# A new order for the attention loop of an attention, mixture-of-experts and SwiGLU kernel

## Chip, cores and metric

The kernel runs on one core of a Trainium2 chip. The metric is the device time of one execution in microseconds. All three stages run in one launch, and the input layouts are prepared before it. Engines are written PE (TensorE, its weight loads apart as PEld), DVE (VectorE), ACT (ScalarE), POOL (GpSimd) and SP (SyncE, which here only issues DMAs).

## Reference

```python
# attention, B=4 H=8 S=576 D=64
scores = (1/sqrt(D)) * q @ k.T
rel = pos[:, None] - pos[None, :]
scores = where((rel >= 0) & (rel < 64), scores, -1e9)
attn = softmax(scores)
x = (attn @ v) -> [2304, 512]
# mixture of experts, N=2304 D=512 E=8 F=1024, top 2
noisy = x @ w_gate + log1p(exp(x @ w_noise)) * noise
top2, weights = softmax over the two largest
y = sum over the token's two experts of weight * (relu(x @ w1[e]) @ w2[e])
# SwiGLU, d_ff=1536
out = (silu(y @ w_gate2) * (y @ w_val2)) @ w_out2
```

## The kernel before

The 2304 tokens are 18 tiles (`NT`) of 128. Three stages follow each other: the attention loop with the gate logits and the routing, the eight experts in order of their token counts, and SwiGLU in six blocks of 384 tokens. Each engine runs its instructions in the order in which the code emits them, so the order of calls in the loop over `T` is the order on each engine. Tiles named with a tag have a fixed number of buffers (`bufs`); a buffer is written again only when all readers of its last content are done.

The attention loop, on which the change bears, works on several tiles at once. In iteration `T`:

- `trans_p(T)` transposes the softmax numerators of tile T on PE (8 matmuls into `ptp`, PSUM banks 4 and 5); ACT copies them to `pt`; DVE forms the reciprocal row sums `rr`.
- `qk(T+2, ...)` adds the mask (2 matmuls with `identb`) and the scores (32 matmuls of 64 rows, `sc`) of tile T+2, in three parts: head pairs 0 and 1, then 2, then 3. The scores of two tiles in work lie in four banks, 0 to 3.
- `softmax(T+2)`: DVE takes row maxima `nm` and scales them to `nms`; ACT makes 8 exponentials.
- `pv(T)`: 32 matmuls into `xp` (bank 6), DVE scales them to `xs`, and a DMA stores `xs` to `x_d` in DRAM, from which tokens are gathered for the experts later.
- `win_v(T+2)`: POOL builds the shifted V block `vw` (2 buffers).
- `trans_x(T-1)` transposes `xs` into `xtp` (also bank 6), ACT copies it to `xt`; `logits(T-2)` multiplies by the gate weights into `misc` (bank 7) and DVE copies to `lts`; `gates(T-2)` holds `trans_l`, which turns `lts` on PE, and a DVE copy to `lg`.
- `route_some(ns)` emits some DVE steps of the routing of a group of five tiles (softplus, top 2, positions in the experts, index lists); a group is opened when `gates` has done its last tile, which is in iterations 6, 11 and 16.
- `split_pair` (iterations 3 to 10): POOL splits one raw weight pair of the first expert into a high part (L114) and the rest (L117), 1024 columns each; SP loads the next raw pair (3 buffers).
- `load_super` loads q, k and v for two tiles (SP); `link_k` is a DVE copy of the last K block of the former pair of tiles into the middle place of the new K tile.

After the loop, a list `TAIL` orders the rest of the attention with the first matmuls of the first expert between it.

Of the kernel before, what the change touches and what calls it, by code (L numbers as in the profile page):

```python
# [7 lines left out]
F32 = mybir.dt.float32  # L8
# [6 lines left out]
ALU = mybir.AluOpType  # L15
# [24 lines left out]

TAIL = ("P16", "L14", "Q14", "R302", "X15", "R1500", "G0", "P17", "V16", "L15", "G1", "W", "V17", "Q15", "R9000", "X16",
        "M0", "L16", "X17", "R9000", "R500", "Q16", "R1", "R2500", "L17", "M2", "W", "R500", "M1", "Q17", "W", "M3",
        "R1500", "E", "R700", "M5", "M6", "M4", "R9000", "E", "W", "R9000", "Y0", "Y1", "M7")
TAIL2 = ("Y2", "Y3")
# [7 lines left out]
def tile_attention_moe_swiglu(ctx: ExitStack, tc: tile.TileContext, qh, kh, vh, wgn, noise, w1h, w2h,  # L54
# [14 lines left out]
    def bank(i, name, shape=None):  # L69
        return ps.tile(shape or [128, 512], F32, name=name, tag=f"b{i}")  # L70
# [32 lines left out]
    def split_pair(pool):  # L103
        j = st["split"]
        if j >= NPAIR:
            return
        while st["load"] < min(j + 3, st["lim"]):
            load_pair()
        st["split"] += 1
        w = pool.tile([128, 2, 1024], F32R, name=f"wp{j}", tag="w")  # L110
        pairs[j] = w
        r = raws.pop(j)
        if st["split"] <= PSPL:
            nc.gpsimd.tensor_scalar(w[:, 0, :], r, 1.0, 0.0, op0=ALU.mult, op1=ALU.add)  # L114
# [166 lines left out]
    with ExitStack() as ac:  # L281
        ap = ac.enter_context(tc.tile_pool(name="ap", bufs=1))

        def load_super(s):
            qt = ap.tile([128, 4, 256], F32, name=f"q{s}", tag="q", bufs=2)
            kt = ap.tile([128, 4, 5, 64], F32, name=f"k{s}", tag="k", bufs=2)
            for h in ((slice(0, 4),) if s else (slice(0, 2), slice(2, 4))):
                cols = slice(0, 256 if s else 128)
                nc.sync.dma_start(qt[:, h, cols], qh[s, :, h, cols])
                nc.sync.dma_start(kt[:, h, 0:2, :], kh[s, :, h, 0:2, :])  # L290
                nc.sync.dma_start(kt[:, h, 3:5, :], kh[s, :, h, 2:4, :])
            if s == 0:
                nc.sync.dma_start(qt[:, :, 128:256], qh[s, :, :, 128:256])
            Q[s], K[s] = qt, kt
            for t in (2 * s, 2 * s + 1):
                V[t] = ap.tile([128, DM], F32, name=f"v{t}", tag="v", bufs=6)
                nc.sync.dma_start(V[t], vh[t])

        def link_k(s):
            if s == 0:  # L300
                nc.vector.memset(K[s][:, :, 2, :], 0.0)
            else:
                nc.vector.tensor_copy(K[s][:, :, 2, :], K[s - 1][:, :, 4, :])

        Q, K, V, VW = {}, {}, {}, {}
        load_super(0)
        wgn_sb = ap.tile([128, NK, 32], F32, name="wgn_sb")
        nc.sync.dma_start(wgn_sb[:, :, 0:16], wgn)
        nc.vector.memset(wgn_sb[:, :, 16:32], 0.0)
        noise_sb = ap.tile([128, NT, E], F32, name="noise_sb")  # L310
        nc.sync.dma_start(noise_sb, noise)
        load_super(1)

        ident4 = ap.tile([128, 16], F32, name="ident4")
        nc.vector.tensor_reduce(ident4, identf.rearrange("p (k c) -> p c k", c=32)[:, 0:16, :], axis=AX.X, op=ALU.add)
# [73 lines left out]
        def qk(T, hps):  # L389
            s, i = divmod(T, 2)  # L390
            mname = {0: "lo", 9: "lo", 4: "up", 13: "up"}.get(T, "mid")
            banks = scb.setdefault(T, [])
            for h2 in range(2 if not banks else 0):
                b_ = bank(2 * (T % 2) + h2, f"sc{T}_{h2}", [128, 4, 128])
                banks.append(b_)
                nc.tensor.matmul(b_, identb, masks[mname][:, None, :].to_broadcast([128, 4, 128]),
                                 start=True, stop=False, skip_group_check=True)
            for hp in hps:
                for blk in range(2):
                    for h2 in range(2):  # L400
# [37 lines left out]
        def pv(T):  # L438
            xb = bank(3 if T == NT - 1 else 6, f"xp{T}", [128, 4, 2, 64])
            for h2 in range(2):  # L440
                for hp in range(4):
                    h = 2 * hp + h2
                    for blk in range(2):
                        vv = VW[T] if blk == 0 else V[T]
                        nc.tensor.matmul(xb[64 * blk:64 * blk + 64, hp, h2, :],  # L445
                                         PT[T][:, h2, hp, 64 * blk:64 * blk + 64],
                                         vv[:, h * 64:h * 64 + 64], start=True, stop=True)
            rr = RR.pop(T)
            xs = ap.tile([128, 4, 2, 64], F32, name=f"xs{T}", tag="xs", bufs=2)
            nc.vector.tensor_tensor(xs, xb, rr.rearrange("p a b -> p b a")[:, :, :, None]  # L450
                                    .to_broadcast([128, 4, 2, 64]), op=ALU.mult)
            XS[T] = xs.rearrange("p a b d -> p (a b d)")
            (nc.scalar if T < RT else nc.sync).dma_start(x_d[T * 128:T * 128 + 128, :], XS[T])

        def trans_x(T):
            b_ = bank(6, f"xtp{T}", [128, 4, 128])
            for k in range(NK):
                transpose(b_[:, k, :], XS[T][:, k * 128:k * 128 + 128])
            xt = ap.tile([128, NK, 128], F32, name=f"xt{T}", tag="xt", bufs=2)
            nc.scalar.activation(xt, b_, AF.Copy)  # L460
            XT[T] = xt
# [180 lines left out]

        for T in range(NT - 2):
            trans_p(T)
            qk(T + 2, (0, 1))
            if T % 2 == 0 and T // 2 + 2 < NT // 2:
                load_super(T // 2 + 2)
            route_some(RNS if T < RT else RNS3)
            if T >= 2:
                logits(T - 2)  # L650
            if T >= 1:
                trans_x(T - 1)
            if T % 2 == 1 and T // 2 + 2 < NT // 2:
                link_k(T // 2 + 2)
            route_pe()
            route_some(RNS2 if T < RT else RNS3)
            qk(T + 2, (2,))
            if T >= 2:
                gates(T - 2)
            qk(T + 2, (3,))  # L660
            softmax(T + 2)
            pv(T)
            win_v(T + 2)
            route_pe()
            if T >= 3 and st["split"] < APAIRS:
                split_pair(wp)
        while routing:
# [441 lines left out]
```

## Time and profile before

| | |
|---|---|
| time, median of 3 runs | 1052.13 us (1051.91 to 1052.77) |
| profiled execution, its own time | 1050.45 us |
| its span, first to last instruction | 1048.7 us |
| PE busy | 1019.6 us, 97% |
| DVE, ACT, POOL busy | 570.3, 340.0, 185.0 us |
| granted TensorE clock, mean | 0.989 |

The span is 1.75 us shorter than the execution's own time, and that execution is 1.68 us under the median. A busy PE is not PE at its peak: at half clock the same matmuls take longer and still count as busy.

### The profile page before, as it was taken

How to read it: one execution, taken by the hardware profiler on the slowest of the kernel's cores; microseconds unless marked ns; L12 is line 12 of the kernel's file. 1: busy time of each engine (PE TensorE's matmuls, PEld its weight loads, DVE VectorE, ACT ScalarE, POOL GpSimd, SP SyncE). 2: the span in 40 equal slices, each digit the busy share in tenths (PEclk: the TensorE clock that was granted, in tenths of full speed). 3: DMA queues.
4: the chain of work that ended last, by engine and by line, in shares of the span. 5: the costliest groups of instructions: out<-in, count | busy, mean ns of one | idle time of the engine just before them, and what ended most of it. 6: DMA issues, size and time to landing. Idle time of an engine off the chain costs nothing.

```text
span 1048.7 us, 16938 instructions
## 1 busy us (share of the span) xinstructions
PE 1019.6 (97%) x6754; PEld 912.6 (87%) x6754; DVE 570.3 (54%) x1155; ACT 340.0 (32%) x808; POOL 185.0 (18%) x232
## 2 busy tenths in 40 slices
PE   8988899999999999999999999999999999999996
PEld 5656788988989898989888899999999999999996
DVE  5688856677878796968543444324324324324321
ACT  6755523423324141424242442212212212212211
POOL 2663114414020101010020151201102102001000
PEclk9988999999999999999999999999999999999999
DMA  7853215657666676756252350201102002000000
GB/s 233 302 192 114 72 51 201 195 196 212 203 205 219 198 230 200 238 183 225 102 187 81 137 171 24 78 1 35 56 1 58 34 1 61 31 1 21 11 1 33
DMA packets 55773, 125.63 MB, mean 120 GB/s; under 512 B 9143, under 2 KB 19511, under 8 KB 55687
## 3 DMA queue, kind: packets, MB, share of 16 engines
q1 hardware_dynamic: 40695, 87.72, 26.0%
q0 software_dynamic: 7936, 23.91, 7.3%
q10 hardware_dynamic: 7056, 12.85, 3.3%
q8 instruction: 55, 0.90, 0.3%
q14 instruction: 31, 0.25, 0.1%
HBM read 95.57 MB, written 28.88 MB: 119 GB/s over the span
## 4 chain that ended last, share of the span: by engine, by line
PE 85%; DVE 7%; DMA 3%; issue 2%; ACT 2%; SPq 1%; ACTq 0%; POOL 0%; DVEq 0%
PE y L270 20%; PE h L248 15%; PE g L958 14%; PE v L958 14%; PE o L986 14%; PE xp L445 2%; PE gt L228 2%; PE ptp L185 1%; PE sc L404 1%; DMA w_d<-da 1%; PE ct L185 1%; DVE wp L117 1%; DMA rd<-in_wg_dram 1%; DVE nm L414 1%; ACT wp L116 1%
## 5 line engine op out<-in xcount | busy, mean ns | idle before, releaser
L270 PE MATMUL y<-wp,ht 128*128 128x512 f32 (+6 forms) x960 | 229.2, 394 | 0.4 <-DVE ht L253 0.4
L248 PE MATMUL h<-xh,wp 128*128 128x256 f32 (+6 forms) x1536 | 219.5, 303 | 2.4 <-DVE ht L253 2.3
L248 PEld LDWEIGHTS h<-xh,wp 128*128 128x128 f32 x1536 | 215.5, 190 | 5.9 <-DVE ht L253 4.3
L270 PEld LDWEIGHTS y<-wp,ht 128*128 128x128 f32 (+6 forms) x960 | 172.4, 183 | 41.2 <-DVE ht L253 0.8
L958 PE MATMUL g<-x,wp 128*128 128x384 f32 x864 | 161.7, 335 | 0.0
L958 PE MATMUL v<-x,wp 128*128 128x384 f32 x864 | 161.3, 334 | 0.0
L986 PE MATMUL o<-wp,ut 128*128 128x512 f32 x648 | 153.6, 393 | 0.0
L958 PEld LDWEIGHTS g<-x,wp 128*128 128x128 f32 x864 | 151.3, 188 | 1.0
L958 PEld LDWEIGHTS v<-x,wp 128*128 128x128 f32 x864 | 150.8, 188 | 0.0
L986 PEld LDWEIGHTS o<-wp,ut 128*128 128x128 f32 x648 | 120.4, 188 | 24.1
L963 DVE TENSOR_TENSOR eg<-g,eg 128x384 f32<-128x384 f32 x72 | 40.2, 558 | 143.7 <-ACT eg L962 143.6
L117 DVE TENSOR_TENSOR wp<-raw,wp 128x1024 fp32r<-128x1024 f32 x67 | 82.0, 1225 | 35.4 <-ACT wp L116 33.9
L250 ACT ACTIVATE ht<-h 128x256 fp32r<-128x256 f32 (+7 forms) x128 | 53.4, 422 | 108.3 <-PE h L248 96.7
L213 POOL DMA_INDIRECT xg<-x_d,idx_i x38 | 36.7, 967 | 283.0 <-PE gt L228 239.7
L966 ACT ACTIVATE ut<-u 128x384 fp32r<-128x384 f32 x72 | 37.8, 525 | 148.2 <-DVE u L965 148.2
L116 ACT ACTIVATE wp<-raw 128x1024 fp32r<-128x1024 f32 x73 | 76.6, 1054 | 24.5 <-DMA raw<-in_w_dram 18.1
L274 ACT ACTIVATE ys<-y 128x512 f32<-128x512 f32 (+6 forms) x40 | 23.8, 596 | 170.1 <-PE y L270 138.0
L962 ACT ACTIVATE eg<-g 128x384 f32<-128x384 f32 x72 | 35.3, 490 | 126.3 <-PE g L958 126.3
L965 DVE TENSOR_TENSOR u<-v,eg 128x384 f32<-128x384 f32 x72 | 40.2, 558 | 62.7 <-PE v L958 62.1
L253 DVE SCALAR_TENSOR_TENSOR ht<-h,ht 128x256 fp32r<-128x256 f32 (+7 forms) x128 | 60.3, 474 | 17.3 <-ACT ht L250 17.3
L693 POOL DMA_INDIRECT gy<-y_d,recp x30 | 28.6, 952 | 214.9 <-DVE xc L700 207.1
L967 DVE TENSOR_TENSOR ut<-u,ut 128x384 fp32r<-128x384 f32 x72 | 41.0, 569 | 43.0 <-ACT ut L966 43.0
(184 smaller groups left out, 937.0 us busy)
## 6 DMA issues: line engine op xcount, KB each, us to landing
raw<-in_w_dram SPq DMA_DIRECT2D x64, 512.0 KB, 4.7
w_d<-da ACTq DMA_DIRECT2D x36, 256.0 KB, 4.6
raw<-w_d SPq DMA_DIRECT2D x18, 512.0 KB, 4.2
y_d<-ys SPq DMA_DIRECT2D x34, 256.0 KB, 2.3
rd<-in_wg_dram SPq DMA_DIRECT2D x12, 512.0 KB, 5.2
rd<-in_wv_dram SPq DMA_DIRECT2D x12, 512.0 KB, 5.5
rd<-in_wo_dram SPq DMA_DIRECT2D x12, 512.0 KB, 4.4
v<-in_v_dram SPq DMA_DIRECT2D x18, 256.0 KB, 6.0
```

The costliest lines, as they stand in the source:

```text
L116: nc.scalar.activation(w[:, 0, :], r, AF.Copy)
L117: (nc.gpsimd if j < PSPL or (j >= WLIM and j % 2) else nc.vector).tensor_tensor(w[:, 1, :], r, w[:, 0, :].bitcast(F32), op=ALU.subtract)
L248: nc.tensor.matmul(b_, w[:, a, k, fc], xh[:, c, k, 0:m], start=(n == 0), stop=(n == 11))
L250: nc.scalar.activation(ht[:, 0, f, 0:m], b_, AF.Relu)
L253: nc.vector.scalar_tensor_tensor(ht[:, 1, f, 0:m], b_, 0.0, ht[:, 0, f, 0:m].bitcast(F32), op0=ALU.max, op1=ALU.subtract)
L270: nc.tensor.matmul(b_, ht[:, a, f, sl], w[:, c, f % 2, :], start=(f == 0 and n == 0), stop=(f == 7 and n == 2))
L958: nc.tensor.matmul(b_, w[:, a, k, fc], x2[:, c, k, :], start=(n == 0), stop=(n == 11))
L963: nc.vector.tensor_tensor(eg, gb[0], eg, op=ALU.mult)
L965: nc.vector.tensor_tensor(u, gb[1], eg, op=ALU.mult)
L966: nc.scalar.activation(ut[:, 0, fi, :], u, AF.Copy)
L967: nc.vector.tensor_tensor(ut[:, 1, fi, :], u, ut[:, 0, fi, :].bitcast(F32), op=ALU.subtract)
L986: nc.tensor.matmul(ob[i], ut[:, a, fi, sl], w[:, c, f % 2, :], start=(f == 0 and n == 0), stop=(f == 11 and n == 2))
```

## The change

The loop over `T` is emitted in another order: the scores of a tile are one batch, `gates(T-2)` comes right after `trans_p(T)`, `trans_x(T-1)` after the scores, and `logits(T-1)`, one tile earlier than before, at the end of the iteration. The scores use three banks in turn instead of four, and `xtp` has bank 3 to itself for the first 16 tiles. The middle K block of a pair is loaded by a DMA from DRAM instead of being copied by DVE. POOL's split runs in pieces of 512 and 256 columns. The `x_d` stores are issued by SP for all tiles (before by ACT for T < 13), and the second pair of q and k is loaded ahead of the first v tiles, the gate weights and the noise.

```diff
-TAIL = ("P16", "L14", "Q14", "R302", "X15", "R1500", ...
+TAIL = ("P16", "Q14", "R302", "X15", "R1500", ...
...
-        if st["split"] <= PSPL:
-            nc.gpsimd.tensor_scalar(w[:, 0, :], r, 1.0, 0.0, op0=ALU.mult, op1=ALU.add)
-        else:
-            nc.scalar.activation(w[:, 0, :], r, AF.Copy)
-        (nc.gpsimd if j < PSPL or (j >= WLIM and j % 2) else nc.vector).tensor_tensor(w[:, 1, :], r, w[:, 0, :].bitcast(F32), op=ALU.subtract)
+        if j < PSPL:
+            for c in range(0, 1024, 512):
+                nc.gpsimd.tensor_scalar(w[:, 0, c:c + 512], r[:, c:c + 512], 1.0, 0.0, op0=ALU.mult, op1=ALU.add)
+            for c in range(0, 1024, 256):
+                sl = slice(c, c + 256)
+                nc.gpsimd.tensor_tensor(w[:, 1, sl], r[:, sl], w[:, 0, sl].bitcast(F32), op=ALU.subtract)
+            return
+        nc.scalar.activation(w[:, 0, :], r, AF.Copy)
+        (nc.gpsimd if j >= WLIM and j % 2 else nc.vector).tensor_tensor(w[:, 1, :], r, w[:, 0, :].bitcast(F32), op=ALU.subtract)
...
+            if s == 0:
+                nc.vector.memset(kt[:, :, 2, :], 0.0)
...
+            else:
+                nc.sync.dma_start(kt[:, :, 2, :], kh[s - 1, :, :, 3, :])
             Q[s], K[s] = qt, kt
+
+        def load_v(s):
             for t in (2 * s, 2 * s + 1):
                 V[t] = ap.tile([128, DM], F32, name=f"v{t}", tag="v", bufs=6)
                 nc.sync.dma_start(V[t], vh[t])
-        def link_k(s):
-            if s == 0:
-                nc.vector.memset(K[s][:, :, 2, :], 0.0)
-            else:
-                nc.vector.tensor_copy(K[s][:, :, 2, :], K[s - 1][:, :, 4, :])
...
         load_super(0)
+        load_super(1)
+        load_v(0)
         wgn_sb = ap.tile([128, NK, 32], F32, name="wgn_sb")
...
-        load_super(1)
+        load_v(1)
...
-                b_ = bank(2 * (T % 2) + h2, f"sc{T}_{h2}", [128, 4, 128])
+                b_ = bank((2 * T + h2) % 3, f"sc{T}_{h2}", [128, 4, 128])
...
-            (nc.scalar if T < RT else nc.sync).dma_start(x_d[T * 128:T * 128 + 128, :], XS[T])
+            nc.sync.dma_start(x_d[T * 128:T * 128 + 128, :], XS[T])
...
-            b_ = bank(6, f"xtp{T}", [128, 4, 128])
+            b_ = bank(3 if T < NT - 2 else 6, f"xtp{T}", [128, 4, 128])
...
         for T in range(NT - 2):
             trans_p(T)
-            qk(T + 2, (0, 1))
-            if T % 2 == 0 and T // 2 + 2 < NT // 2:
-                load_super(T // 2 + 2)
             route_some(RNS if T < RT else RNS3)
             if T >= 2:
-                logits(T - 2)
-            if T >= 1:
-                trans_x(T - 1)
-            if T % 2 == 1 and T // 2 + 2 < NT // 2:
-                link_k(T // 2 + 2)
+                gates(T - 2)
+            if T % 2 == 0 and T // 2 + 2 < NT // 2:
+                load_super(T // 2 + 2)
+                load_v(T // 2 + 2)
+            qk(T + 2, range(4))
             route_pe()
             route_some(RNS2 if T < RT else RNS3)
-            qk(T + 2, (2,))
-            if T >= 2:
-                gates(T - 2)
-            qk(T + 2, (3,))
+            if T >= 1:
+                trans_x(T - 1)
             softmax(T + 2)
             pv(T)
+            route_pe()
+            if T >= 1:
+                logits(T - 1)
             win_v(T + 2)
-            route_pe()
             if T >= 3 and st["split"] < APAIRS:
                 split_pair(wp)
```

**PE, one tile of the loop.** Before, from one transpose of numerators to the next `pv`; `misc<-xt` is `logits`, `misc<-ident,lts` is `trans_l`:

```order
L185 MATMUL ptp_0_765<-identf,p_615 128x128 x4
L185 MATMUL ptp_1_771<-identf,p_615 128x128 x4
...
L404 MATMUL sc_1_782<-k_490,q_489 64x128
L466 MATMUL misc<-xt_708,wgn_sb 32x128 x4
L185 MATMUL xtp_798<-identf,xs_753 128x128 x4
L404 MATMUL sc_0_780<-k_490,q_489 64x128
...
L473 MATMUL misc<-ident_150,lts_796 128x16
L404 MATMUL sc_0_780<-k_490,q_489 64x128
...
L445 MATMUL xp_832<-vw_648,pt_764 64x64
```

In the changed kernel the same stretch, up to the end of the iteration:

```order
L189 MATMUL ptp_0_879<-identf,p_728 128x128 x4
L189 MATMUL ptp_1_885<-identf,p_728 128x128 x4
L479 MATMUL misc<-ident_152,lts_864 128x16
...
L402 MATMUL sc_1_908<-mmid,identb 128x512
L410 MATMUL sc_0_906<-k_689,q_688 64x128
...
L189 MATMUL xtp_930<-identf,xs_857 128x128 x4
L451 MATMUL xp_953<-vw_767,pt_878 64x64
...
L472 MATMUL misc<-xt_935,wgn_sb 32x128 x4
```

The scores are no longer cut in three; `trans_l` stands ahead of them and `logits` behind `pv`.

**DVE, where the routing of the first group begins.** Before, from the `xs` of tile 7 on (`dd` to `mf` are routing steps; `lts` is what `trans_l` waits for):

```order
L450 TENSOR_TENSOR xs_1059<-xp_1042,rr_977 128x512
L434 TENSOR_SCALAR rr_1083<-rs_922 128x8
L435 RECIPROCAL rr_1083<-rr_1083 128x8
L496 TENSOR_TENSOR dd_1012<-dd_1012,ru_1014 128x40
L499 TENSOR_TENSOR nz_1108<-lnu_994,dd_1012 128x40
L501 TENSOR_TENSOR nz_1108<-nz_1108,noise_sb 128x40
L503 TENSOR_TENSOR nz_1108<-nz_1108,lg 128x40
L508 MAX mx_all<-nz_1108 128x8 x5
L511 MAX_INDEX mi_1112<-mx_all,nz_1108 128x8
L468 COPY lts_1123<-misc 128x128
L511 MAX_INDEX mi_1112<-mx_all,nz_1108 128x8 x4
L514 CAST mf_all<-mi_1112 128x10
```

In the changed kernel, from the `xs` of tile 6 on:

```order
L456 TENSOR_TENSOR xs_970<-xp_953,rr_891 128x512
L474 COPY lts_977<-misc 128x128
L440 TENSOR_SCALAR rr_1004<-rs_826 128x8
L441 RECIPROCAL rr_1004<-rr_1004 128x8
L494 TENSOR_SCALAR u_1007<-ez_926 128x40
L497 SCALAR_TENSOR_TENSOR dd_1009<-u_1007,ez_926 128x40
L500 RECIPROCAL ru_1011<-u_1007 128x40
L502 TENSOR_TENSOR dd_1009<-dd_1009,ru_1011 128x40
L505 TENSOR_TENSOR nz_1014<-lnu_928,dd_1009 128x40
L507 TENSOR_TENSOR nz_1014<-nz_1014,noise_sb 128x40
L480 COPY lg<-misc 128x16
L509 TENSOR_TENSOR nz_1014<-nz_1014,lg 128x40
```

`lts` now stands right behind `xs`, ahead of the routing steps.

**POOL, iterations 4 and 5.** Before, the V blocks and one split:

```order
L383 TENSOR_SCALAR vw_756<-v_494 64x512
L387 TENSOR_SCALAR vw_756<-v_329 64x512
L114 TENSOR_SCALAR wp_761<-raw_653 128x1024
L117 TENSOR_TENSOR wp_761<-raw_653,wp_761 128x1024
L383 TENSOR_SCALAR vw_852<-v_496 64x512
```

In the changed kernel:

```order
L389 TENSOR_SCALAR vw_767<-v_491 64x512
L393 TENSOR_SCALAR vw_767<-v_318 64x512
L115 TENSOR_SCALAR wp_772<-raw_659 128x512 x2
L118 TENSOR_TENSOR wp_772<-raw_659,wp_772 128x256 x4
L389 TENSOR_SCALAR vw_866<-v_493 64x512
```

Two instructions became six; their place did not move.

## Rows read from the trace of the kernel before

**Rows 1.** The page: busy time, share of the span and instructions of each engine.

```profile
PE 1019.6 (97%) x6754; PEld 912.6 (87%) x6754; DVE 570.3 (54%) x1155; ACT 340.0 (32%) x808; POOL 185.0 (18%) x232
```

**Rows 2.** Busy time by stretch: start:end, length, engines; granted clock, DMA share, GB/s.

```profile
15.10:42.82 27.72, 26.87 (x433) 19.95 (x431) 17.79 (x45) 21.91 (x95) 12.27 (x14) 0.94 0.82 277
42.82:89.73 46.91, 37.07 (x533) 27.46 (x533) 38.09 (x99) 27.04 (x116) 28.49 (x25) 0.85 0.52 181
89.73:114.02 24.29, 23.20 (x383) 17.14 (x379) 19.58 (x80) 17.91 (x78) 4.91 (x8) 0.93 0.33 111
```

**Rows 3.** The same view: first and last of the five half-clock stretches.

```profile
15.20:18.60 3.40, 3.40 (x40) 3.28 (x41) 3.09 (x8) 2.39 (x14) 1.23 (x2) 0.50 0.95 299
...
90.30:93.70 3.40, 3.40 (x40) 3.03 (x36) 2.60 (x8) 2.84 (x17) 1.23 (x2) 0.50 0.76 235
```

**Rows 4.** Timeline of PE, one tile without routing: start, length, what.

```profile
27.69 1.09 PE L185 MATMUL ptp<-identf,p 128*128 128x128 f32 x8
28.62 0.59 PE L396 MATMUL sc<-mmid,identb 128*128 128x512 bf16 x2
29.15 0.67 PE L404 MATMUL sc<-k,q 64*64 64x128 f32 x16
29.74 0.42 PE L466 MATMUL misc<-xt,wgn_sb 128*32 128x128 f32 x8
30.10 0.66 PE L185 MATMUL xtp<-identf,xs 128*128 128x128 f32 x4
30.69 0.45 PE L404 MATMUL sc<-k,q 64*64 64x128 f32 x8
31.07 0.40 PE L473 MATMUL misc<-ident,lts 128*128 128x16 f32 x2
31.39 0.45 PE L404 MATMUL sc<-k,q 64*64 64x128 f32 x8
32.02 0.24 PE L445 MATMUL xp<-vw,pt 128*64 128x64 f32 x1 [0.18 <-ACT xt L460]
33.10 1.09 PE L185 MATMUL ptp<-identf,p 128*128 128x128 f32 x8
```

**Rows 5.** Timeline of PE: the scores of one tile in one batch.

```profile
7.72 1.10 PE L404 MATMUL sc<-k,q 64*64 64x128 f32 x32 [0.52 <-DMA q<-in_q_dram]
```

**Rows 6.** Waits of PE, 15.1 to 120 us: total, times, longest.

```profile
PE misc L473 <- DVE lts L468: 9.4, 5, 3.3
```

**Rows 7.** Timeline of DVE: three slow instructions, and one that ran free.

```profile
41.24 2.40 DVE L303 COPY k<-k 128x256 f32<-128x256 f32 x1
...
75.86 0.77 DVE L546 SCALAR_TENSOR_TENSOR pp<-tl,pos_all 128x10 f32<-128x10 f32 x1
76.75 2.81 DVE L554 TENSOR_TENSOR ohk<-iok,key 128x480 f16<-128x480 f16 x1
...
106.43 0.65 DVE L554 TENSOR_TENSOR ohk<-iok,key 128x480 f16<-128x480 f16 x1
```

**Rows 8.** Timeline of POOL at the times of the slow ones.

```profile
41.13 2.36 POOL L117 TENSOR_TENSOR wp<-raw,wp 128x1024 fp32r<-128x1024 f32 x1
...
75.57 1.04 POOL L114 TENSOR_SCALAR wp<-raw 128x1024 fp32r<-128x1024 f32 x1
76.70 2.35 POOL L117 TENSOR_TENSOR wp<-raw,wp 128x1024 fp32r<-128x1024 f32 x1
```

**Rows 9.** POOL's groups, 15.1 to 114.02 us: count, busy, mean ns, idle before.

```profile
L117 POOL TENSOR_TENSOR wp<-raw,wp 128x1024 fp32r<-128x1024 f32 x8 | 18.8, 2356 | 0.7
...
L383 POOL TENSOR_SCALAR vw<-v 64x512 f32<-64x512 f32 x15 | 9.2, 612 | 51.6 <-PE xp L445 30.5 <-issue 21.1
L114 POOL TENSOR_SCALAR wp<-raw 128x1024 fp32r<-128x1024 f32 x8 | 8.4, 1050 | 0.7
```

**Rows 10.** Timeline of SP (DMA issues): length holds the wait.

```profile
23.99 2.29 SPq L101 DMA_DIRECT2D raw<-in_w_dram  x3
...
38.16 5.68 SPq L101 DMA_DIRECT2D raw<-in_w_dram  x2
```

More of the change, by code (lines that the diff above doesn't have):

```diff
@@ L39 @@
 EVP = {16: "da", 17: "da"}
-TAIL = ("P16", "L14", "Q14", "R302", "X15", "R1500", "G0", "P17", "V16", "L15", "G1", "W", "V17", "Q15", "R9000", "X16",
+TAIL = ("P16", "Q14", "R302", "X15", "R1500", "G0", "P17", "V16", "L15", "G1", "W", "V17", "Q15", "R9000", "X16",
         "M0", "L16", "X17", "R9000", "R500", "Q16", "R1", "R2500", "L17", "M2", "W", "R500", "M1", "Q17", "W", "M3",
@@ L621, in route_until @@
                 pass
-        link_k(0)
-        link_k(1)
         for T in range(2):
@@ L644, in tile_attention_moe_swiglu @@
             trans_p(T)
-            qk(T + 2, (0, 1))
+            route_some(RNS if T < RT else RNS3)
+            if T >= 2:
+                gates(T - 2)
             if T % 2 == 0 and T // 2 + 2 < NT // 2:
                 load_super(T // 2 + 2)
-            route_some(RNS if T < RT else RNS3)
-            if T >= 2:
-                logits(T - 2)
+                load_v(T // 2 + 2)
+            qk(T + 2, range(4))
+            route_pe()
+            route_some(RNS2 if T < RT else RNS3)
             if T >= 1:
                 trans_x(T - 1)
-            if T % 2 == 1 and T // 2 + 2 < NT // 2:
-                link_k(T // 2 + 2)
-            route_pe()
-            route_some(RNS2 if T < RT else RNS3)
-            qk(T + 2, (2,))
-            if T >= 2:
-                gates(T - 2)
-            qk(T + 2, (3,))
             softmax(T + 2)
             pv(T)
+            route_pe()
+            if T >= 1:
+                logits(T - 1)
             win_v(T + 2)
-            route_pe()
             if T >= 3 and st["split"] < APAIRS:
```

## Prediction

> **What bounds the kernel now.** I read the page first: PE is busy for 1019.6 of 1048.7 us [rows 1], so any time in which PE does not wait, or runs faster, is time off the end, and no other engine sets the pace over the whole. The change touches the attention loop and little else. So I cut the loop into three stretches between starts of `pv` and read the engines' busy time in each [rows 2]: tiles 0 to 5 (27.72 us), 5 to 11 (46.91 us), 11 to 15 (24.29 us). The reader is to see that the middle stretch costs 7.8 us a tile against 5.5 and 6.1 in the others, with PE idle for 9.8 us of it, DVE busy for 38.09 and a granted clock of 0.85.
>
> Next I looked at a tile without routing [rows 4]. From one `ptp` at 27.69 to the next at 33.10 it is 5.41 us, and PE stops once, for 0.18 us. Such a tile is bound by PE at full clock. Then I asked who makes PE wait elsewhere: `trans_l` waiting for the DVE copy `lts`, 9.4 us in 5 waits, the longest 3.3 [rows 6]. On DVE the copy stands behind a run of routing steps, and some of those steps are far too long. A product `ohk` of 480 columns takes 2.81 us at 76.75 and 0.65 at 106.43; the K copy at 41.24 takes 2.40 [rows 7]. Each of the long ones lies beside a POOL split: the copy ends at 43.64, POOL's at 43.49; `ohk` ends at 79.56, POOL's at 79.05 [rows 8]. DVE stood still until POOL's instruction was over. At 75.86 `pp` ends at 76.63, just behind POOL's first piece (76.61), while POOL's second had not begun: DVE gets in between two POOL instructions.
>
> Last, the clock. PE ran at a granted 0.50, its level of 1.2 GHz, in five stretches (four of about 3.4 us, one of 6.8), of which the first and the last are shown [rows 3]. Each came while or after PE had waited. A stretch of 3.4 us at half clock gives 1.7 us less work.
>
> **The change part by part.**
>
> *PE's order and banks.* Before, the scores of a tile are batches of 16, 8 and 8, which take 0.59, 0.38 and, with the wait, 0.63 us from start to start; the wait is `pv` for ACT's read of `xtp`, since both use bank 6 [rows 4]. All 32 in one batch took 1.10 us, of which 0.07 overlaps the next (0.67 against 0.60 to 0.59 for the 16) [rows 5]: 1.03 us. So the batch saves 0.59 + 0.38 + 0.38 - 1.03 = 0.32 us, and bank 3 for `xtp` removes another 0.25. A plain tile becomes 5.41 - 0.57 = 4.84 us on PE. ACT has 21.91 us of work in five tiles [rows 2], 4.4 a tile, and now runs close behind; I take 4.95. In the first stretch the first tile holds a half-clock stretch: 27.72 - 4 x 5.41 = 6.08, which I leave; four tiles gain 0.46 each: **-1.8 us** (bounds 0 and -2.3).
>
> Three score banks instead of four add a wait: the second mask of tile T+2 needs the first four exponentials of tile T+1. PE comes back to that mask 0.59 + 1.08 + 0.35 + 0.93 + 0.32 + 0.27 = 3.5 us after the end of a tile's scores [rows 4]; in that time DVE takes one maximum, and ACT, which needs 4.4 us for a tile's eight exponentials and three copies, makes four exponentials, at most half of that. Price 0; if DVE is late by over 1 us it shows as a wait of PE on ACT, but `trans_l` would then wait about as long.
>
> *`lts` ahead of the routing.* This takes away the serial pattern in which DVE routes while PE waits and PE works while DVE waits. Now `trans_l` of iteration T waits for a copy that DVE makes right behind `xs` in iteration T-1; the routing steps fall into PE's 3 us of transposes, masks and scores. What is late next is DVE itself: a tile cannot be shorter than DVE's work in it. With routing but without splits DVE has 19.58 us in four tiles, 4.9 a tile; without routing 17.79 in five, 3.6 [rows 2]. In the middle stretch four of six iterations hold routing (7 to 10), so DVE's own work would be 4 x 4.9 + 2 x 3.6 = 26.8 us, and of its 38.09 some 11.3 are standing still behind POOL.
>
> *K link by DMA.* Seven such copies lie in the three stretches; they leave DVE, and with them their part of those 11.3 us. The DMA writes 128 KB a pair of tiles on SP's queue; what hides it is that pairs are loaded two iterations ahead.
>
> *Short pieces.* POOL's split takes 1050 + 2356 ns now, a `vw` of half the columns 612 [rows 9]. A piece of 512 columns is thus about 0.61 us; a piece of 256 columns of the second kind lies between 2356/4 = 0.59 and, with a fixed part of 0.17 (2 x 612 - 1050 = 174 ns), 0.72. With gaps of 0.08 a split becomes 4.0 to 4.5 us instead of 3.5, and POOL 5.4 to 5.9 us a tile with its two `vw` pieces. One DVE step now waits at most some 0.7 us instead of 2.36, but a run of steps can meet a piece each, and POOL is there longer. Bounds for the middle stretch: no waiting at all, and all 11.3 us as before. Between ends so far apart I go by the rows in which steps come in runs (`pp`, then `ohk`, both caught) and take 8.7. The stretch is then 2 x 4.95 + 4 x 4.95 + 8.7 = 38.4 us: **-8.5 us** (bounds -17.2 and -5.9). I add nothing for the clock: PE will still wait there and will still be halved at times, but when DVE sets the pace a slower PE costs little.
>
> *Last stretch.* No splits, routing of the second group, one half-clock stretch before [rows 3]. Four tiles at 4.95 would be 19.8; the steps are unevenly dealt (from iteration 13 on more per call), so I take 5.5 a tile, 22.0: **-2.3 us** (bounds -4.5 and 0).
>
> *After the loop.* `L14` is done in the loop, and one of the five waits for `lts`, about 1 us, lies there: **-1.0 us** (bounds 0 and -1.5). Behind it the stages are PE's and only shift.
>
> *SP's queue, load order.* Stores and loads now share one queue in order. Before, SP ran ahead and issued the first three raw loads at 24 us [rows 10]; now they stand behind the store of `xs` of tile 3, which I put at 33. POOL's first split starts some 3 us later, and SP already stands 5.68 us in two raw loads that wait for a POOL split [rows 10]; behind them stand the next q and k. I work out that these land 2 to 4 us before they are needed. Price 0, bounds below. The earlier second q and k shorten PE's first waits, but ACT's exponentials of the first tiles then gate `pv`; price 0 (bounds -1 and +0.5).
>
> **Sum:** -1.8 - 8.5 - 2.3 - 1.0 = -13.6 us. The profiled execution took 1050.45 us, so 1036.9; it was 1.68 us under the median of the runs shown, so on that scale 1038.5 us.
>
> **Rivals.**
>
> *A, the sum above:* 1033.5 to 1044. Chance 0.54.
>
> *B, the pieces free DVE.* If DVE's steps find gaps, the middle tiles go at 4.95 (29.7, -17.2) and the last ones too (-4.5): -24.5 in all. But then POOL is next: eight tiles at 5.4 to 5.9 us instead of 4.95 give back 3.6 to 7.6. That leaves about -19 us: 1033. For it speaks the 0.77 us of `pp`; against it the length of the runs. Chance 0.20.
>
> *C, POOL becomes the bound.* If DVE's steps hold up POOL as well, POOL's tile is 5.9 us plus about 1.5 to 2 of DVE steps, 7.4 to 7.9, for eight tiles: the middle keeps its 7.8 us a tile, and -1.8, -1.0 and about -1 remain: 1048. Against it: POOL's 2.35 and 2.36 us beside waiting DVE steps show no such stretch [rows 8]. Chance 0.10.
> The Trainium skill's page "SBUF — State Buffer", section "Who interferes with whom", states that DVE and POOL take a shared pair of ports as an exclusive lock for a whole instruction, and that whichever comes second is blocked fully. By that rule C's mechanism holds both ways; this trace agrees with it for DVE (2.40 and 2.81 us) and does not show it for POOL.
>
> *D, slower: SP's queue starves PE.* Three loads of q and k (iterations 4, 6, 8) stand behind a raw load that waits for POOL. If each lands after its use by t, PE waits 3t. The gain is gone at t = 4.5 us; at 6 us it is +18 - 13.6 = +4.4: 1056.5. It needs POOL some 8 us behind. For it: 5.68 us of standing now [rows 10], longer splits. Against it: a tile in this stretch is 6 to 7 us by A, which gives POOL time. Chance 0.11.
>
> *No measurable change,* parts of C and D together: 0.05. About 0.2%, 2.1 us, is what a measurement of this kernel can tell from none.
>
> **How the numbers follow.** The likeliest is A, 1038.5. From B's 1033 less 2 for its own bounds up to C's 1048 plus 2 holds over 8 in 10: 1031 to 1050. Faster: A, B and C, 0.84; same 0.05; slower 0.11.
>
> **What would show it.** Right: one score batch of about 1.03 us and no wait of `pv` for `xt`; plain tiles near 4.95 us; no `trans_l` wait over 1.5 us; DVE steps beside splits at 0.4 to 0.9 us instead of 2.4; the stretch from tile 5 to 11 near 38 us. Wrong: PE waiting for q or k after 40 us (D), for `vw` (C, B's limit), or for ACT at the second mask; or half-clock stretches as many as before with DVE not late.

## The result, and the profile after

The changed kernel takes 1040.94 us (median of 4 executions, 1039.68 to 1041.54) against 1052.45 us before (1051.91 to 1053.13): a ratio of 0.9889, 95% interval 0.9872 to 0.9906. That is 11.5 us faster, 2.4 us above the predicted 1038.5 and inside the range. The profiled execution took 1041.45 us with a span of 1039.5.

The page's busy line of the changed kernel answers to [rows 1]:

```profile
PE 1011.3 (97%) x6754; PEld 907.7 (87%) x6754; DVE 563.2 (54%) x1147; ACT 340.3 (33%) x808; POOL 191.7 (18%) x268
```

PE's busy time fell by 8.3 us with the same 6754 matmuls; POOL has 36 instructions and 6.7 us more.

Next, the busy time by stretch, cut as in [rows 2] at the starts of `pv` of tiles 0, 5, 11 and 15:

```profile
16.47:39.67 23.20, 22.98 (x430) 17.83 (x431) 16.15 (x44) 21.67 (x95) 7.62 (x13) 1.00 0.74 237
39.67:80.74 41.07, 33.03 (x544) 24.58 (x544) 34.95 (x96) 27.52 (x118) 39.10 (x58) 0.92 0.82 269
80.74:103.03 22.29, 19.94 (x371) 15.07 (x370) 18.82 (x78) 17.86 (x76) 6.09 (x9) 1.00 0.40 126
```

The three stretches last 23.20, 41.07 and 22.29 us instead of 27.72, 46.91 and 24.29. The loop begins later, 16.47 against 15.10. In the first stretch PE is idle for 0.22 us. The middle one is still the costly one, 6.8 us a tile, and POOL is now busy for 39.10 of its 41.07 us.

The timeline of PE in one tile without routing, against [rows 4]:

```profile
26.79 0.43 PE L472 MATMUL misc<-xt,wgn_sb 128*32 128x128 f32 x8
27.15 1.09 PE L189 MATMUL ptp<-identf,p 128*128 128x128 f32 x8
28.08 0.29 PE L479 MATMUL misc<-ident,lts 128*128 128x16 f32 x2
28.22 0.59 PE L402 MATMUL sc<-mmid,identb 128*128 128x512 bf16 x2
28.74 1.10 PE L410 MATMUL sc<-k,q 64*64 64x128 f32 x32
29.78 0.66 PE L189 MATMUL xtp<-identf,xs 128*128 128x128 f32 x4
30.36 0.27 PE L451 MATMUL xp<-vw,pt 128*64 128x64 f32 x1
```

One batch of scores takes 1.04 us from its start to that of `xtp`, `pv` follows `xtp` after 0.58 with no wait, and the starts of `pv` in the first stretch (21.06, 25.71, 30.36, 35.02, 39.67) are 4.65 us apart.

The waits of PE from 16.4 to 112 us, the four largest, against the 9.4 us of [rows 6]:

```profile
PE misc L479 <- DVE lts L474: 6.8, 7, 2.2
PE misc L479 <- DVE idx_f L583: 1.3, 1, 1.3
PE sc L410 <- DMA k<-in_k_dram: 1.3, 1, 1.3
PE misc L479 <- DVE idx_f L587: 1.1, 1, 1.1
```

The wait for `lts` is smaller in sum, its longest 2.2 instead of 3.3. Some of it is now put down to `idx_f`, a routing step on DVE. New is a wait for a K block.

DVE's timeline beside two splits, against the slow steps of [rows 7]:

```profile
64.31 0.97 DVE L560 TENSOR_TENSOR ohk<-iok,key 128x480 f16<-128x480 f16 x1
...
67.16 0.68 DVE L420 TENSOR_REDUCE nm<-sc 128x4 f32<-128x512 f32 x1
...
70.70 3.27 DVE L566 TENSOR_TENSOR ohp<-iop,pp 128x256 f16<-128x256 f16 x4
```

And POOL's timeline: the second part of a split without routing steps beside it, then of the two splits beside these steps; against [rows 8, 9]:

```profile
38.13 2.79 POOL L118 TENSOR_TENSOR wp<-raw,wp 128x256 fp32r<-128x256 f32 x4
...
64.72 3.79 POOL L118 TENSOR_TENSOR wp<-raw,wp 128x256 fp32r<-128x256 f32 x4
...
71.07 3.49 POOL L118 TENSOR_TENSOR wp<-raw,wp 128x256 fp32r<-128x256 f32 x4
```

`ohk` takes 0.97 instead of 2.81 us. But a step still waits: 0.65 was its free time in [rows 7]. And now POOL waits too: its four pieces take 3.79 and 3.49 us beside DVE's steps, 2.79 without them. The four `ohp` steps take 3.27 us while POOL makes its four pieces. Taken one by one, the steps start at 70.70, 71.30, 72.16 and 73.03 and the pieces at 71.07, 71.92, 72.79 and 73.66: the engines take turns.

### The profile page after: what moved, and what is told of

It reads as the page before. It is cut to its first block, busy times and chain, and to the rows that moved or that the text cites. A ratio compares the mean times of both kernels' runs of the same rounds, so it can differ in the third digit from the quotient of the medians.

```text
span 1039.5 us, 16954 instructions
## 1 busy us (share of the span) xinstructions
PE 1011.3 (97%) x6754; PEld 907.7 (87%) x6754; DVE 563.2 (54%) x1147; ACT 340.3 (33%) x808; POOL 191.7 (18%) x268
## 4 chain that ended last, share of the span: by engine, by line
PE 88%; DVE 6%; issue 2%; DMA 2%; SPq 1%; ACT 1%; POOL 0%; ACTq 0%; DVEq 0%
PE y L274 20%; PE h L252 18%; PE g L959 14%; PE v L959 14%; PE o L987 14%; PE gt L232 2%; PE sc L410 1%; DVE nm L420 1%; DVE xs L456 1%; PE ct L189 1%; DMA k<-in_k_dram 1%; PE xp L451 1%; PE xtp L189 0%; DMA v<-in_v_dram 0%; PE sc L402 0%
```

## The experiments

Each kernel is compared with the kernel before on the same chip, in the same series. The theory that I set out with, O in the expectations: the new order of the loop with its banks carries most of the gain, the short pieces a smaller part, and the splits still cost most of what is left. The rivals: the pieces carry the gain (P), or the K link by DMA or the load order has a part in it.

| kernel | edit | us | before there | ratio, 95% interval | profiled span |
|---|---|---|---|---|---|
| the change | | 1040.94 | 1052.45 | 0.9889 (0.9872 to 0.9906) | 1039.5 |
| `a_long` | change, long splits | 1046.22 | 1052.57 | 0.9938 (0.9920 to 0.9956) | 1044.4 |
| `a_dvelink` | change, K link by DVE | 1040.63 | 1052.57 | 0.9882 (0.9864 to 0.9901) | 1039.5 |
| `b_order` | before, new order and banks | 1047.29 | 1052.57 | 0.9948 (0.9927 to 0.9969) | 1046.3 |
| `b_pieces` | before, short pieces | 1046.80 | 1052.57 | 0.9952 (0.9937 to 0.9967) | 1043.0 |
| `a_nosplit` | change, 7 of 8 splits left out | 1032.12 | 1052.95 | 0.9808 (0.9786 to 0.9831) | 1029.9 |
| `b_nosplit` | before, 7 of 8 splits left out | 1038.17 | 1052.95 | 0.9864 (0.9837 to 0.9890) | 1036.4 |
| `a_bank` | change, a fourth bank for tile 1 | 1039.31 | 1052.95 | 0.9870 (0.9851 to 0.9889) | 1038.6 |
| `a_raw` | change, fewer raw loads at first | 1041.85 | 1052.95 | 0.9893 (0.9868 to 0.9918) | 1039.2 |
| `a_early` | change, splits two iterations earlier | 1037.61 | 1050.50 | 0.9871 (0.9850 to 0.9891) | 1036.1 |
| `a_plain` | `a_bank`, splits away from most routing | 1035.88 | 1050.50 | 0.9856 (0.9835 to 0.9877) | 1032.9 |
| `a_p128` | change, pieces half as long | 1036.16 | 1050.50 | 0.9868 (0.9849 to 0.9887) | 1032.7 |
| `a_both` | `a_plain`, last three splits as in `a_p128` | 1035.18 | 1048.96 | 0.9866 (0.9845 to 0.9887) | 1032.2 |

**The pieces, taken out and put in alone.** `a_long` gives the changed kernel the old split; `b_pieces` is the reverse edit on the kernel before.

```diff
-        if j < PSPL:
-            for c in range(0, 1024, 512):
-                nc.gpsimd.tensor_scalar(w[:, 0, c:c + 512], r[:, c:c + 512], 1.0, 0.0, op0=ALU.mult, op1=ALU.add)
-            for c in range(0, 1024, 256):
-                sl = slice(c, c + 256)
-                nc.gpsimd.tensor_tensor(w[:, 1, sl], r[:, sl], w[:, 0, sl].bitcast(F32), op=ALU.subtract)
-            return
...
+        if st["split"] <= PSPL:
+            nc.gpsimd.tensor_scalar(w[:, 0, :], r, 1.0, 0.0, op0=ALU.mult, op1=ALU.add)
...
+        (nc.gpsimd if j < PSPL or (j >= WLIM and j % 2) else nc.vector).tensor_tensor(w[:, 1, :], r, w[:, 0, :].bitcast(F32), op=ALU.subtract)
```

> The changed kernel with POOL's splits long again (1024 columns, two instructions), nothing else undone. Theory O (the order of the loop carries most of the gain, short pieces a smaller part): about 1044 us, 1042 to 1047; the stretch from tile 5 to 11 some 3 us longer than the 41.1 of the changed kernel, single DVE steps of 2.3 us back. Rival P (the pieces carry the gain, since DVE standing behind POOL is what made the loop slow): 1048 us or more.

> The kernel before with the short POOL pieces alone. Theory O: 2 to 4 us of gain, about 1049: the longest waits of DVE shrink from 2.1 us to 0.6, but the serial pattern of the order stays. Rival P: 6 us of gain or more, 1046 or less.

Taken out of the change, the pieces cost 0.0049 of the time, 5.3 us (1046.22 - 1040.94); put in alone they give 1052.57 - 1046.80 = 5.8 us. `a_long` lies in the 1042 to 1047 of theory O; the gain of `b_pieces` lies above O's 2 to 4 us and just under the 6 of rival P, so the pieces are worth more than I had thought. PE's largest wait in `a_long`, and there DVE's `ohk`, POOL's one long instruction, and a small DVE step beside POOL's next split:

```profile
PE misc L475 <- DVE lts L470: 10.0, 6, 4.2
```

```profile
66.30 2.83 DVE L556 TENSOR_TENSOR ohk<-iok,key 128x480 f16<-128x480 f16 x1
```

```profile
66.25 2.36 POOL L117 TENSOR_TENSOR wp<-raw,wp 128x1024 fp32r<-128x1024 f32 x1
```

```profile
72.41 1.81 DVE L417 TENSOR_SCALAR nms<-nm 128x4 f32<-128x4 f32 x1
```

With long pieces the 2.8 us step is back, it ends half a microsecond behind POOL's (69.13 against 68.61), `nms` takes 1.81 us where 0.17 is its free time, and PE waits 4.2 us for the `lts` behind both, longer than before the change.

**The order alone.** `b_order` is the kernel before with the new order of calls, three score banks and bank 3 for `xtp`; splits, link, stores and loads stay.

```diff
             trans_p(T)
-            qk(T + 2, (0, 1))
...
+                gates(T - 2)
...
+            qk(T + 2, range(4))
...
-            qk(T + 2, (2,))
...
-            qk(T + 2, (3,))
...
+                logits(T - 1)
```

> The kernel before with the new order of the loop and the new banks alone: long splits, K link by DVE, stores on ACT, first loads as before. Theory O: half of the gain or more, about 1046 us (1044 to 1048). Rival P: at most 2 us of gain, 1050 to 1053, since DVE still stands behind the long splits.

It gains 5.3 us, as theory O had it. With 5.8 from `b_pieces` that is 11.1 of the 11.5 us: the two add up, and 0.4 is left for the link, the stores and the load order together. The intervals of the three ratios, some 2 us each, leave room for about 3 us either way. Its largest wait is longer than any of the kernel before:

```profile
PE misc L473 <- DVE lts L468: 13.6, 9, 5.0
```

So the order alone saves PE's own time and pays in waits behind long splits; the pieces take those waits down again. The stretches show where each half works, here the first two of `b_order` and the middle one of `b_pieces`:

```profile
16.73:40.50 23.77, 23.11 (x431) 17.87 (x431) 18.51 (x46) 21.66 (x95) 12.15 (x14) 1.00 0.87 307
40.50:85.99 45.49, 33.11 (x544) 24.49 (x543) 38.91 (x99) 27.21 (x118) 28.39 (x25) 0.85 0.57 187
```

```profile
42.39:81.40 39.01, 32.14 (x533) 23.12 (x533) 32.35 (x96) 26.68 (x116) 33.52 (x50) 0.98 0.64 218
```

The order alone takes 4.0 us off the first stretch and only 1.4 off the middle one. The pieces alone take nothing off the first (27.69 against 27.72) and 7.9 off the middle. The change's middle, 41.07, is 2.1 us longer than that of `b_pieces`: beside short pieces the new order seems to give some of it back there. The middles of four kernels close to the change (the change, `a_raw`, `a_dvelink`, `a_bank`) lie between 41.07 and 42.28, so this difference is little more than such kernels differ by.

**The K link back on DVE.**

```diff
-                nc.sync.dma_start(kt[:, :, 2, :], kh[s - 1, :, :, 3, :])
...
+            nc.vector.tensor_copy(K[s][:, :, 2, :], K[s - 1][:, :, 4, :])
```

> The changed kernel with the middle K block copied by DVE again, pieces kept. Theory O: each of 8 copies costs DVE 0.3 us and up to 0.7 us of standing behind a piece; in the tiles in which DVE sets the pace this shows, about +2 us: 1043. Rival (the link is hidden either way): 1041, within 1 us of the changed kernel.

No difference, against the 2 us of theory O and with its rival, and the waits of PE agree: there is no wait for K left, and more for `lts` (8.4 against 6.8):

```profile
PE misc L481 <- DVE lts L476: 8.4, 6, 3.0
```

**The splits left out.** In both kernels the weight pairs 1 to 7 are not split and pair 0 stands in for them; their loads stay.

```diff
+        if 1 <= j < APAIRS:
+            pairs[j] = pairs[0]
+            raws.pop(j)
+            return
```

> The changed kernel with seven of POOL's eight splits of the loop left out: the weight pairs 1 to 7 of the first expert are replaced by pair 0 (the raw pairs are still loaded), so the first expert's result is not the reference's. What POOL still costs DVE in the changed kernel. Theory (DVE still stands behind pieces, by the piece): the stretch from tile 5 to 11 falls from 41.1 to 30 to 32 us, the total by 8 to 10 us, 1031 to 1033. Rival (the short pieces have already freed DVE; what is left is DVE's own work): within 3 us of the changed kernel, 1038 to 1041.

> The kernel before with the same seven splits left out. All of DVE's standing behind long splits is gone, the order is the old one: by the 11.3 us of standing that the prediction took, 1041 to 1044. If the serial pattern of the old order costs most, only 1046 or more.

Before, the splits cost 14.8 us (1052.95 - 1038.17), more than the 9 to 12 of the expected 1041 to 1044. In the change they still cost 8.8 (1040.94 - 1032.12, medians of two series; by the ratios, 0.9889 - 0.9808, it is 8.5), inside the expected range. The middle stretch of `a_nosplit`, then that of `b_nosplit`:

```profile
39.46:71.80 32.34, 29.92 (x545) 22.44 (x544) 26.18 (x96) 27.27 (x118) 9.69 (x16) 1.00 1.01 336
```

```profile
42.45:75.27 32.82, 31.51 (x533) 22.86 (x534) 25.82 (x97) 26.52 (x116) 7.38 (x12) 1.00 0.74 243
```

In `a_nosplit` it lasts 32.34 instead of 41.07 us, PE stays at full clock, and DVE's 34.95 us become 26.18: 8.77 us of DVE's busy time beside splits was standing still. In `b_nosplit` it lasts 32.82 instead of 46.91, and DVE's 38.09 become 25.82. So without splits the old and the new order are level in this stretch. DVE's timeline in `a_nosplit`, with the four `ohp` steps that took 3.27 us above:

```profile
64.22 1.38 DVE L570 TENSOR_TENSOR ohp<-iop,pp 128x256 f16<-128x256 f16 x4
```

**The prologue's bank.**

```diff
-                b_ = bank((2 * T + h2) % 3, ...)
+                b_ = bank(3 if (T, h2) == (1, 1) else (2 * T + h2) % 3, ...)
```

> The changed kernel with one bank moved: the second score half of tile 1 goes to bank 3, so that it does not wait for the first exponentials of tile 0 (2.26 us of PE at 9.39 us). Theory (this wait put the start of the loop 1.4 us later than before): the first pv at 15.1 us instead of 16.47, and about -1.4 us at the end. Rival (the first pv is held by the landing of v and the V block on POOL as well): less than 0.5 us.

The first `pv` starts at 15.62 instead of 16.47, not at the 15.1 of my theory. The time is 0.002 lower by the ratios, less than the width of the intervals, so it decides neither for the theory nor for the rival. The wait that this takes away, on PE in the changed kernel, and the one that stands at the next step in `a_bank`:

```profile
9.39 0.58 PE L402 MATMUL sc<-mmid,identb 128*128 128x512 bf16 x1 [2.26 <-ACT p L423]
```

```profile
9.07 1.99 PE L410 MATMUL sc<-k,q 64*64 64x128 f32 x32 [1.68 <-DMA q<-in_q_dram]
```

With the bank free PE waits 1.68 us for a q block instead, and the scores of tile 1 start at 9.07 instead of 9.91: of the 2.26 us the bank itself cost 0.84.

**The raw loads.**

```diff
-        while st["load"] < min(j + 3, st["lim"]):
+        while st["load"] < min(j + (3 if j else 1), st["lim"]):
```

> The changed kernel with only the first raw weight pair loaded in iteration 3; the second and third follow one iteration later, behind q, k and v of tiles 8 and 9. Theory (1.25 us of PE at 44.45 us is the K link landing late behind 1.5 MB of weights): that wait goes, about -1.5 us. Rival: POOL then lacks its raw pair and its V blocks come late, no gain.

No gain. The changed kernel's SP queue and PE at the K wait:

```profile
27.65 5.00 SPq L459 DMA_DIRECT2D x_d<-xs  x2
32.70 1.66 SPq L101 DMA_DIRECT2D raw<-in_w_dram  x3
```

```profile
44.45 0.78 PE L410 MATMUL sc<-k,q 64*64 64x128 f32 x20 [1.26 <-DMA k<-in_k_dram]
```

In `a_raw` the wait is gone here and a like one stands at 56.37:

```profile
PE sc L410 <- DMA k<-in_k_dram: 1.4, 1, 1.4
```

PE also waits 0.8 us for `vw`, as the rival had it. I read this so that a raw load moved out of the way of one pair of tiles is in the way of the next; no run tests it.

**Where the splits stand, and how long a piece is.** Three kernels of one series, then one that joins two of them. `a_plain` and `a_both` have the moved bank of `a_bank` as well.

```diff
-            if T >= 3 and st["split"] < APAIRS:
+            if T >= 1 and st["split"] < APAIRS:              # a_early
+            if T in (1, 2, 3, 4, 5, 6, 10, 11):              # a_plain
```

> The changed kernel with its eight splits begun two iterations earlier: at the ends of iterations 1 to 8, not 3 to 10. Six then lie beside tiles without routing, two beside routing. Theory (a split costs by the DVE routing steps it lies beside): leaving out the splits took 8.7 us off the stretch from tile 5 to 11, nearly all of it in tiles 7 to 10, so two of the four there bring back about 4 us; in the tiles without routing POOL now has 4.1 + 1.2 = 5.3 us against PE's 4.65, which costs at most 0.7 us in each of the first ones: 1037 to 1039.5, with PE waiting for vw in tiles 2 to 6. Rival (POOL's own time per tile is the bound wherever the splits stand): what is won in the middle is lost in the first stretch, 1040.5 to 1042. Second rival (raw loads that stand ahead of q and k on SP's queue): PE waits for q or k before 30 us, 1043 or more.

> The changed kernel with the splits at the ends of iterations 1 to 6, 10 and 11, and tile 1's second score half in bank 3. Theory: none of the splits lies beside the tiles 7 to 9, and one (behind tile 11) beside a tile without routing: 1041 less 8.7 for the middle, plus 1.2 for tile 10, plus 2 to 3 for POOL's 5.3 us a tile in the first stretch, less 1 for the bank: about 1035, range 1033 to 1037. Rival (POOL is the bound wherever the splits stand): 1039 to 1041.

```diff
-            for c in range(0, 1024, 512):
+            for c in range(0, 1024, 256):
...
-            for c in range(0, 1024, 256):
-                sl = slice(c, c + 256)
+            for c in range(0, 1024, 128):
+                sl = slice(c, c + 128)
```

> The changed kernel with pieces half as long again: 256 columns for the first part of a split, 128 for the second, twelve pieces instead of six. From 1.05 for 1024 columns, 0.62 for 512, and 2.35 for 1024 against 0.73 for 256 of the second kind I estimate 0.39 and 0.46 us a piece, 5.2 us a split instead of 4.1. Theory M (the two engines share the time that both want, and a split costs by its whole length): some 1 us more beside each of the four routing tiles: 1043 to 1045. Rival N (a DVE step waits for one piece, and half the piece is half the wait): 1037.5 to 1039.5.

In microseconds `a_early` and `a_plain` came out where the theory had them: 1037.61 in 1037 to 1039.5, 1035.88 in 1033 to 1037. But the kernel before was 2 us lower on that chip. By the ratios, 0.9871 and 0.9856, they would be at 1038.9 and 1037.3 beside the change's 1040.94, the second just outside its range. Against the change's 0.9889 only `a_plain` differs by more than the two intervals allow together (0.0033 against 0.0027), and barely; `a_early`, `a_p128` and `a_both` do not. What follows rests on the stretches. Those of `a_plain`:

```profile
14.12:39.09 24.97, 23.17 (x431) 17.89 (x431) 15.85 (x44) 21.78 (x95) 17.21 (x28) 1.00 0.94 300
39.09:75.55 36.46, 31.42 (x545) 23.42 (x544) 29.60 (x96) 27.32 (x118) 23.73 (x38) 0.95 0.86 273
```

The middle is 4.6 us shorter than the change's, the first stretch 1.8 longer and the last, 24.40 us, 2.1. In `a_early` the middle is 3.2 us shorter (37.89) and the first 1.8 longer (25.00). But the reason that I gave for the price in the first stretch, PE waiting for `vw`, is not there: beside `lts` PE waits in `a_plain` for K blocks, 2.9 us, of which 1.4 lie in the first stretch and 1.5 in the middle; in `a_early` it waits 1.1 for K in the first. I put that down to the raw loads, which now stand earlier in SP's queue; no run takes them out:

```profile
PE misc L479 <- DVE lts L474: 6.2, 6, 2.5
PE sc L410 <- DMA k<-in_k_dram: 2.9, 2, 1.5
```

For `a_p128` rival N was right, by the ratio 1038.6 in its 1037.5 to 1039.5, and theory M, which I had put first, wrong. DVE's steps beside its splits, and below POOL's pieces where the four `ohp` have just ended:

```profile
61.40 0.74 DVE L560 TENSOR_TENSOR ohk<-iok,key 128x480 f16<-128x480 f16 x1
...
66.08 2.55 DVE L566 TENSOR_TENSOR ohp<-iop,pp 128x256 f16<-128x256 f16 x4
```

```profile
69.98 3.36 POOL L118 TENSOR_TENSOR wp<-raw,wp 128x128 fp32r<-128x128 f32 x8
```

`ohk` is at 0.74, close to its free 0.65, and four `ohp` take 2.55 instead of 3.27 (1.38 without splits). POOL needs 3.36 us for eight pieces where four took 2.79. The stretches of `a_p128`:

```profile
38.23:74.67 36.44, 31.17 (x545) 23.52 (x544) 28.19 (x96) 27.47 (x119) 35.50 (x79) 0.95 0.88 281
74.67:98.86 24.19, 19.85 (x370) 15.10 (x370) 21.11 (x80) 17.86 (x76) 17.04 (x35) 1.00 0.46 151
```

4.6 us less in the middle, with POOL busy for 35.50 of 36.44, and 1.9 more in the last stretch, into which POOL's work now reaches. PE waits there for `vw`:

```profile
PE xp L451 <- POOL vw L393: 2.3, 2, 1.5
```

That is rival B of the prediction in kind, though not in size: the steps find gaps, and POOL is next. PE's longest wait in `a_p128` is another one, 2.3 us for a K block in the middle stretch.

Part of what these kernels gain on the change lies behind the loop. From the start of `pv` of tile 15 to the end the change takes 936.5 us, `a_early` 934.6, `a_plain` 933.0, `a_p128` 933.8 and `a_both` 934.1. That is 3.5 of the 6.6 us between the profiled spans of the change and `a_plain`, 2.6 of the 6.8 for `a_p128` and 1.9 of the 3.4 for `a_early`. The change has stops of PE there that these four lack (see "After the loop" below). Up to `pv` of tile 15 the gain is 3.1 us for `a_plain`, 4.2 for `a_p128` and 1.5 for `a_early`.

> The kernel a_plain (splits at the ends of iterations 1 to 6, 10 and 11; tile 1's second score half in bank 3) with the last three splits, those beside routing, in pieces of 256 and 128 columns, as in a_p128. Theory (beside routing the length of a POOL piece sets how long DVE waits, and in tiles without routing it does not matter): the tile behind 7 falls from 9.66 to about 6.1 us and the one behind 12 from 7.41 to about 6.2, as in a_p128; with a_plain's profiled 1034.98 less 4.5 that is 1030.5, range 1029 to 1033, a ratio of about 0.981. Rival (the tile behind 7 is long because POOL has fallen behind over five splits in a row, not because of its pieces): 1034 to 1036, with PE waiting for vw or for lts there as before.

`a_both` missed: 1035.18, a ratio of 0.9866 against the expected 0.981, no better than its two parents. Tile 12 to 13 did fall from 7.41 to 6.21 us as expected, but 7 to 8 only from 9.66 to 7.74. Its timeline of POOL, and DVE's at that time:

```profile
49.15 2.79 POOL L119 TENSOR_TENSOR wp<-raw,wp 128x256 fp32r<-128x256 f32 x4
```

```profile
49.37 0.55 DVE L495 TENSOR_SCALAR u<-ez 128x40 f32<-128x40 f32 x1
49.95 0.67 DVE L498 SCALAR_TENSOR_TENSOR dd<-u,ez 128x40 f32<-128x40 f32 x1
```

The fifth split, still in pieces of 256, lies beside the first routing steps, because POOL runs behind the iteration that emits it: both my theory and its rival are in part right. Of the 83.17 us from `pv` 0 to 15 (85.83 in `a_plain`) the 2.7 us gained do show; later starts and the time after the loop take most of it back in the profiles (spans 1032.9 and 1032.2).

## Why the prediction was right

**The mechanism** held in three of its parts: DVE stood still behind long POOL instructions (`a_long`, `b_nosplit`), short pieces let it in (`b_pieces`), and PE's plain tile shrank (`b_order`). A fourth, `lts` ahead of the routing, is not shown to gain in the middle stretch: without splits the old order takes 32.82 us there and the new one 32.34, and beside long splits PE's waits for `lts` grew from 9.4 to 13.6 us. The experiments add what the sum could not tell: order and pieces are each worth about 5.5 us, the link and the loads nothing that the intervals show.

**The sum, term by term,** in the profiled executions:

| term | predicted | measured |
|---|---|---|
| before the first `pv` | 0 (-1 to +0.5) | +1.4 |
| first stretch | -1.8 | -4.5 |
| middle stretch | -8.5 | -5.8 |
| last stretch | -2.3 | -2.0 |
| from the last stretch on | -1.0 | +1.8 |
| sum | -13.6 | -9.2 |

The profiled spans differ by 9.2 us (1039.5 - 1048.7), the medians by 11.5: the profiled execution of before took 2.0 us less than its median (1050.45 and 1052.45), that of the change 0.5 more (1041.45 and 1040.94). Single executions of one kernel differ by a microsecond or two, so differences of that size between two profiles show nothing.

That the total came so near is in part luck. The first stretch gave 2.7 us more than its term and the middle 2.7 less, and by the profiles, in which the terms are measured, the sum is missed by 4.4 us.

**First stretch and start** belong together: -3.1 for -1.8. A plain tile is 4.65 us, not 4.95. Of the 0.19 us below my 4.84 for PE, 0.18 are `trans_l`, 0.14 us to the next start where it took 0.32 [rows 4]; and the margin of 0.11 for ACT was not needed (21.67 us in 23.20). The price of 0 for three banks was wrong, though, and the start came out beyond the +0.5 that I had given it. I worked the price out for the loop, where it holds: from the first `pv` on, the longest wait at a mask is 0.22 us. Before the loop, with nothing between the scores of tiles 0 and 1, PE waits 2.26 us; `a_bank` puts 0.84 of it down to the bank, and a q block holds PE next. The half-clock stretch that I left in the first stretch moved ahead of it:

```profile
8.90:15.80 6.90, 6.13 (x59) 4.23 (x62) 2.18 (x6) 4.71 (x28) 2.35 (x4) 0.51 1.11 343
56.70:60.10 3.40, 3.35 (x52) 2.73 (x45) 2.86 (x15) 1.24 (x3) 3.24 (x7) 0.50 0.90 298
70.40:73.80 3.40, 3.40 (x38) 2.23 (x38) 3.37 (x6) 2.12 (x10) 3.40 (x6) 0.50 0.83 258
```

These windows of the changed kernel hold all its stretches at 1.2 GHz until well after the loop, three where [rows 3] showed the first and last of five. Each comes after or among waits of PE.

**Middle stretch,** a miss of 2.7 us. The price of 8.7 us for standing behind POOL's pieces came out: `a_nosplit` takes 8.73 us off. That it fits so closely is luck, since I picked it between 0 and 11.3 and did not work it out. The 11.3 itself was a little low: `b_nosplit` takes 12.3 us off DVE's busy time and 14.1 off the stretch. What was clearly too low is the rest: six tiles without splits take 32.34, not 29.7. Of these 2.6 us, 1.3 are the wait for a K block, in tile 5 to 6; tile 6 to 7 gives 0.3 back; and the next four take 5.34, 5.53, 5.16 and 5.37 instead of 4.95, 1.6 together, by DVE's routing steps and PE's waits of up to 0.6 us for `lts`. I had DVE's mean per tile and took the larger of two means; the steps are dealt unevenly. "No `trans_l` wait over 1.5 us" failed accordingly: 2.2. What the fewer half-clock windows give in this stretch, beside the shorter waits that bring them, no run separates.

**Rival C's mechanism** is there, small. By POOL's rows of the changed kernel, four pieces beside DVE's steps take up to 1.0 us more; over 32 pieces the mean is 784 ns, against 2790 / 4 = 698 without: 2.8 us of POOL's time in all. The rule that the prediction weighed, of the Trainium skill's page "SBUF — State Buffer", section "Who interferes with whom", has the lock both ways, and the trace now agrees. The same section says that a reduction never contends for the shared ports on trn2, which fits `nm`, 0.68 us beside a piece and 0.69 at 20.54 with none.

**Rival D** had its place right (SP's queue, raw loads ahead of K behind a store) and its size low: t was over its use by 1.3 us, once, not three times. My working had these loads landing 2 to 4 us early; the change, `a_raw`, `a_plain` and `a_both` show one or two that land late, and where.

**After the loop** the sign was wrong. From `pv` of tile 15 to 17 it takes 8.83 us instead of 8.09, with waits of 0.34 for `xt`, 0.53 for `lts` and 0.36 that the profile calls issue. The waits of PE over the whole span have three more stops called issue, in the first matmuls of the second expert:

```profile
PE h L252 <- issue: 1.7, 3, 1.0
```

With the 0.36 they make 2.1 us, where the kernel before has none. They are enough for the wrong sign; without them the term would be about -0.3, still short of -1.0. The longest of them lies at 191.08, 1.02 us. It stands in `a_bank`, `a_long`, `a_dvelink`, `b_pieces` and both kernels without splits too (0.88 to 1.03 us), in two parts in `b_order` and `a_raw`, and not in the kernel before, `a_early`, `a_plain`, `a_p128` and `a_both`. What the engine lacked there the profile does not name; it stays open.

## What to carry to other kernels

When two engines that block each other work side by side, cut the instructions of the one off the critical path to about the length of the other's, and count then what the cut engine has left: at 256 columns DVE still waited, at 128 PE waited for POOL's `vw`. Placing such work beside tiles that don't need the other engine took as much off the middle stretch as cutting it finer, 4.6 us each, and both paid part of it back in other stretches; the two together gained no more in the total. Price a prologue apart from the loop: a bank or a queue that has slack in the steady state need not have it where nothing lies between two tiles.

## What the runs showed of the hardware

DVE and POOL take turns at instruction boundaries: four `ohp` steps and four pieces of 256 columns interleave one for one, and both become longer. It is not every DVE instruction. Steps with an input in PSUM (`nm` 0.68, `xs` 0.69, `lts` 0.28) keep their times beside a piece, and so does the small reciprocal of `rr` from SBUF (0.20). The small scaling `nms` from SBUF to SBUF, 0.17 us free, doesn't: it took 0.67 at 67.88, and 1.81 beside a long instruction in `a_long`. A piece of half the columns costs POOL more than half: 0.42 us for 128 columns, 0.70 for 256, 2.36 for 1024. PE stops of 0.2 to 1.0 us have no releaser in the profile, 2.1 us in sum in the changed kernel, and come and go with edits far from them.
